# Attention and two MLPs on one core: unit 1's weight split taken out of the attention periods, first loads ahead of the branch

## The chip, the cores and the metric

One NeuronCore of a Trainium2 chip runs the whole program. The metric is the device time of one launch in microseconds (us). Engine names: PE is TensorE (PEld its weight loads), DVE is VectorE, ACT is ScalarE, POOL is GpSimd, SP is SyncE, which here only issues DMAs. A name with a q at its end (PEldq, SPq) is the engine's sequencer, or the DMA issues of its queue.

## The reference, cut to what matters

```python
# attention: batch 2, 12 heads, 448 tokens, head_dim 64, cap = 30
scores = (q @ k.T) / sqrt(64)
scores = cap * tanh(scores / cap)
attn = exp(scores - max(scores)); attn = attn / (sum(attn) + 1e-9)
x = attn @ v                                   # reshaped to 896 x 768
# first MLP, 768 -> 768 -> 768
x = max(x @ w1, x @ w2, x @ w3) @ moe_w_out
# second MLP, 768 -> 1536 -> 768
xn = x / sqrt(mean(x * x) + 1e-6) * rms_g
out = (silu(xn @ w_gate) * (xn @ w_val)) @ moe2_w_out
```

## The kernel before

The program reads the bits of `cap` into a register of every engine (line 630) and branches on them (line 631). With a cap of at most 40 the bounded variant runs, which needs no maximum of the scores; this is the variant in the trace.

**Attention** works on 12 pairs of heads (6 pairs in each of 2 batches), one after the other in `period(i)`, a software pipeline. In period i: SP loads pair i+2; DVE finishes the sum of pair i-1 (`sum_2`, L246), after `norm(i-2)` (the reciprocal, L270, and the product xs, L272), and then writes x of pair i-2 as a high and a low part (`split_x`, L280 and L281); PE computes the transposed scores of pair i (L220, L226), the products with V of pair i-1 (`values`, L260), and the row sums of pair i-1 by a product with ones (`sum_all`, L266); ACT takes tanh of the scores (L222, L229) and then their exponentials (`expo`, L233, two instructions). POOL begins the sum of exponentials (`sum_01`, L237, and `sum_3`, two instructions on L242) as soon as ACT has the exponentials; DVE does this for pairs 0 and 11. Each engine runs its instructions in the order in which the code wrote them. PE can begin the scores of pair i+1 only behind `sum_all(i-1)`, which waits for DVE's `sum_2(i-1)`, which waits for POOL's sums of pair i-1.

**The MLPs** are matmuls in float32r with each operand in two parts. Weights come as 60 units of 128 x 768. Each unit is loaded twice by SP (`raw`, and `mid`, the same bytes shifted by two), and DVE and ACT make a high and a low part of it in eight steps (`split_unit`, L109 to L117), after which the next unit's loads are issued. In attention only units 0 to 2 are split: unit 0 in period 0 in one piece, all on DVE; unit 1 by a list `steps`, of which periods 2 to 8 emit one step each, behind `split_x`, and period 9 the rest; unit 2 in `tail`. `tail` runs as a hook inside the first MLP group, after its 18 matmuls: it is period 12 (the last values and sums), the split of unit 2, and the norm and split of the last pair. Three groups on batch 0 (units 0, 1, 2) follow each other, then three on batch 1. From there on a table by group numbers says when each later unit is split.

**At the start**, behind the branch, ACT loads cap, SP loads K and Q of pair 0, DVE clears a tile, PE multiplies it with itself three times (L329, 448 columns each), and ACT runs one exponential, which loads the table.

Of the kernel before, what the change touches and what calls it, by code (L numbers as in the profile page):

```python
# [1 line left out]

# [16 lines left out]
B, H, S, D = 2, 12, 448, 64  # L19
NP = H // 2  # L20
P = 128
# [8 lines left out]
NT = B * S  # L30
NS = NT // P
U = 768
# [4 lines left out]
CAP_BITS = 0x42200000  # L37


@with_exitstack  # L40
def attn_moe_kernel(ctx, tc, bounded, qT, kT, v, cap, w123, wo, wgv, wo2, rms_g, out):
    nc = tc.nc
    pe, dve, act, pool, sp = nc.tensor, nc.vector, nc.scalar, nc.gpsimd, nc.sync

    const = ctx.enter_context(tc.tile_pool(name="const", bufs=1))
    gp = ctx.enter_context(tc.tile_pool(name="gp", bufs=1))
    wp = ctx.enter_context(tc.tile_pool(name="wp", bufs=1))
    tp = ctx.enter_context(tc.tile_pool(name="tp", bufs=1))
    pp = ctx.enter_context(tc.tile_pool(name="pp", bufs=1, space=PSUM))

    NG, NE, NT, NX = 28, 6, 6, 3

    BATCH, WIDE = (slice(0, S), slice(S, B * S)), (slice(0, 512), slice(512, B * S))
    AHEAD, SPACE, T_MIN = 3, 2, 2
# [2 lines left out]
        return gp.tile([P, 2, S], dt, tag="g", name=name, bufs=NG)  # L57

    def small(name, dt=F32):
        return tp.tile([P, 512], dt, tag="t", name=name, bufs=NT)  # L60

    def flat(name, in_quad=False):

# [11 lines left out]
    def bank():  # L75
        return pp.tile([P, 512], F32, tag="b", name="bank", bufs=5)
# [15 lines left out]

    def load_unit(src):
        raw = wp.tile([P, U, 2], U32, tag="raw", name="raw", bufs=2)
        mid = wp.tile([P, U, 2], U32, tag="mid", name="mid", bufs=2)
        sp.dma_start(out=raw.rearrange("p a b -> p (a b)"), in_=src.bitcast(U32))
        sp.dma_start(out=mid.rearrange("p a b -> p (a b)").bitcast(U16)[:, :4 * U - 2], in_=src.bitcast(U16)[:, 1:4 * U - 1])
        return raw[:, :, 1], mid[:, :, 0]  # L100

    def split_unit(words, on_dve, defer=None):
        hi, lo = (gp.tile([P, U], F32R, tag="g", name=name, bufs=NG) for name in ("whi", "wlo"))
        f = wp.tile([P, U], U32, tag="f", name="f", bufs=2)
        d = wp.tile([P, U], U32, tag="d", name="d", bufs=1)
        high, mid = words
        ff = f.bitcast(F32)
        steps = [
            (lambda: dve.tensor_scalar(f, high, 0x7FFFFFFF, None, op0=ALU.bitwise_and)) if on_dve else  # L109
            (lambda: act.activation(ff, high.bitcast(F32), AF.Abs)),  # L110
            lambda: dve.tensor_scalar(ff, ff, W_MIN, W_MAX, op0=ALU.max, op1=ALU.min),  # L111
            lambda: dve.tensor_scalar(f, f, 3, 0x3FFFF000, op0=ALU.logical_shift_left, op1=ALU.bitwise_and),  # L112
            lambda: dve.scalar_tensor_tensor(f, high, 0xC0000000, f, op0=ALU.bitwise_and, op1=ALU.bitwise_or),  # L113
            lambda: (dve.tensor_copy if on_dve else act.copy)(hi, ff),  # L114
            lambda: dve.tensor_scalar(d, f, 0xFF800000, None, op0=ALU.bitwise_and),
            lambda: dve.tensor_scalar(mid, mid, 0x01FFFFFF, None, op0=ALU.bitwise_and),
            lambda: dve.scalar_tensor_tensor(lo, mid, 2.0 ** -36, d.bitcast(F32), op0=ALU.mult, op1=ALU.mult),  # L117
            load_next,
        ]
        if defer is None:  # L120
            for step in steps:
                step()
        else:
            defer.extend(steps)
        return hi, lo

    unit_src = [w123[j, n] for j in range(KC) for n in range(3)]
# [1 line left out]
    unit_src += [wgv[f, n] for f in range(FC) for n in range(2)]  # L129
    unit_src += [wo2[half, k2] for half in range(2) for k2 in range(FC // 2)]  # L130
    U_WO, U_GV, U_O2 = 3 * KC, 4 * KC, 4 * KC + 2 * FC
    loaded, units = [], []

    def load_next():
        if len(loaded) < len(unit_src):
            loaded.append(load_unit(unit_src[len(loaded)]))

    def split_next(defer=None):
        i = len(units)
        units.append(split_unit(loaded[i], i < 2, defer))  # L140
        loaded[i] = None

    with tc.manual_schedule():

        pairs = [(b, hp) for b in range(B) for hp in range(NP)]
        n = len(pairs)
        kq, vt, E, EX, Ssum, SB, PO, XS, done = {}, {}, {}, {}, {}, {}, {}, {}, {}
# [8 lines left out]
        def load_pair(i):  # L156

            b, hp = pairs[i]
            k_, qv = tp.tile([P, S], F32, tag="k", name="k", bufs=3), big("qv")
            kq[i], vt[i] = (k_, qv[:, 0]), qv[:, 1]  # L160
            sp.dma_start(out=k_, in_=kT[b, hp])
            sp.dma_start(out=qv[:, 0], in_=qT[b, hp])
# [105 lines left out]
        def norm(i):  # L268
            r = small("r")[:, :S]
            dve.reciprocal(r, SB.pop(i)[:, :S])  # L270
            xs = XS[i] = spare()
            dve.tensor_mul(xs, PO.pop(i)[:, :S], r)  # L272

        def split_x(i):
            b, hp = pairs[i]
            if b == 0:
                X[hp] = flat("x")
            hi, lo = (t[:, BATCH[b]] for t in X[hp])
            xs = XS.pop(i)
            dve.tensor_copy(hi, xs)  # L280
            dve.tensor_sub(lo, xs, hi.bitcast(F32))  # L281
# [32 lines left out]
                two_parts(t, *(h[:, cols] for h in HT[j]))  # L314


        cap_sb = const.tile([P, 1], F32, name="cap_sb")
        g_sb = const.tile([P, KC], F32, name="g_sb")
        tsc = const.tile([P, 1], F32, name="tsc")
        act.dma_start(out=cap_sb, in_=cap.to_broadcast([P, 1]))  # L320
        load_pair(0)


        warm = small("warm")[:, :S]
        dve.memset(warm, 0.0)
        act.activation(tsc, warm[:, :1], AF.Exp)
        ps = bank()
        for _ in range(3):
            pe.matmul(ps[:, :S], warm[:, :P], warm, start=True, stop=True)  # L329
        load_next()  # L330
        load_pair(1)
        load_v(0)
# [11 lines left out]
        if bounded:  # L344

            guard = const.tile([P, 1], F32, name="guard")
            dve.tensor_scalar_mul(guard, cap_sb, -1.0)
            dve.tensor_tensor(guard, guard, cap_sb, op=ALU.min)
            act.activation(guard, guard, AF.Exp)
            dve.tensor_scalar_mul(guard, guard, 1e-9 / P)  # L350
            steps = []

            def period(i):

                if i + 2 < n:
                    load_pair(i + 2)
                    load_v(i + 2)
                if i >= 2:  # L360
                    norm(i - 2)
                if i == n:
                    sum_3(i - 1, dve)
                if i >= 1:
                    sum_2(i - 1)
                if i >= 2:
                    split_x(i - 2)

                    if i == 2:
                        split_next(steps)  # L370
                    for step in steps[:1 if i < 9 else None]:
                        step()
                    del steps[:1 if i < 9 else None]
                if i == 1:
                    scores(1, 0)
                    scores(1, 1)
                    values(0, 0, 1)
                    scores(1, 2)
                    scores(1, 3)
                    values(0, 2)  # L380
                    sum_all(0)
                else:
                    if i < n:
                        for c in range(NC):
                            scores(i, c)
                    if i >= 1:
                        values(i - 1, *(() if i < n else (3,)), 0, 1, 2)
                        sum_all(i - 1)
                if i < n:
                    expo(i)  # L390
                    if i == 0:

                        split_next()
                        sum_01(i, dve)
                        sum_3(i, dve)
                    else:
                        sum_01(i, dve if i == n - 1 else pool)
                        if i < n - 1:
                            sum_3(i, pool)

            def tail():
                period(n)
                split_next()
                norm(n - 1)
                split_x(n - 1)

            for i in range(n):
                period(i)
        else:
            for i in range(n):  # L410
                if i + 2 < n:
                    load_pair(i + 2)
                    load_v(i + 2)
                attend(i)
            for _ in range(3):
                split_next()
# [220 lines left out]
```

## Time and profile before

| | us |
|---|---|
| median of 3 runs | 552.27 (549.04 to 552.77) |
| profiled execution | 551.83 |
| its span in the trace | 550.0 |
| PE busy | 530.8 (97%) |
| DVE busy | 423.2 (77%) |
| ACT busy | 240.3 (44%) |
| POOL busy | 61.3 (11%) |

The span begins and ends inside the launch, 1.83 us shorter than it. Attention reaches from 0 to about 103 us, the MLPs from there to the end. Busy time counts an instruction from its begin to its end, its waiting for a port included. PE's busy time is that of overlapping instructions, so that a busy PE may still be slow.

### The profile page before, as it was taken

How to read it: one execution, taken by the hardware profiler on the slowest of the kernel's cores; microseconds unless marked ns; L12 is line 12 of the kernel's file. 1: busy time of each engine (PE TensorE's matmuls, PEld its weight loads, DVE VectorE, ACT ScalarE, POOL GpSimd, SP SyncE). 2: the span in 40 equal slices, each digit the busy share in tenths (PEclk: the TensorE clock that was granted, in tenths of full speed). 3: DMA queues.
4: the chain of work that ended last, by engine and by line, in shares of the span. 5: the costliest groups of instructions: out<-in, count | busy, mean ns of one | idle time of the engine just before them, and what ended most of it. 6: DMA issues, size and time to landing. Idle time of an engine off the chain costs nothing.

```text
span 550.0 us, 7028 instructions
## 1 busy us (share of the span) xinstructions
PE 530.8 (97%) x2684; PEld 436.0 (79%) x2684; DVE 423.2 (77%) x592; ACT 240.3 (44%) x347; POOL 61.3 (11%) x48
## 2 busy tenths in 40 slices
PE   7996996999999999999999999999999999999996
PEld 3332332489988889988998999998888899999996
DVE  4699999999898898776686888887877778836701
ACT  4996895523434333435454343333333333312301
POOL 0367367000000000003122000000000000000000
PEclk9999999999999999999999999999999999999999
DMA  7932231048897878676400587666666666974402
GB/s 251 371 104 71 86 122 59 0 121 282 297 333 286 283 241 280 234 258 229 141 0 1 174 260 238 221 212 213 208 207 222 227 222 209 327 275 168 162 1 106
DMA packets 24809, 105.89 MB, mean 193 GB/s; under 512 B 3008, under 2 KB 9408, under 8 KB 24768
## 3 DMA queue, kind: packets, MB, share of 16 engines
q1 hardware_dynamic: 23760, 104.19, 55.7%
q10 hardware_dynamic: 1008, 1.18, 0.6%
q8 instruction: 23, 0.38, 0.3%
q14 instruction: 18, 0.15, 0.1%
HBM read 102.60 MB, written 2.75 MB: 192 GB/s over the span
## 4 chain that ended last, share of the span: by engine, by line
PE 87%; DVE 6%; ACT 5%; POOL 1%; issue 1%; DVEq 0%; POOLq 0%
PE bank L290 40%; PE banko L290 16%; PE bank L558 10%; PE banks L290 7%; PE banko L558 3%; ACT e L222 3%; PE bank L220 2%; PE banks L558 2%; ACT e L233 2%; PE banko L260 2%; DVE sum L246 2%; DVE r L270 2%; PE banks L266 1%; PE bank L329 1%; DVE x L280 1%
## 5 line engine op out<-in xcount | busy, mean ns | idle before, releaser
L114 ACT CAST whi<-f 128x768 fp32r<-128x768 f32 x58 | 48.8, 841 | 148.4 <-DVE f L113 139.1
L290 PE MATMUL bank<-xn,whi 128*128 128x512 f32 (+1 forms) x360 | 102.9, 367 | 0.0
L290 PE MATMUL bank<-x,whi 128*128 128x512 f32 (+2 forms) x276 | 79.2, 368 | 0.0
L290 PEld LDWEIGHTS bank<-xn,whi 128*128 128x128 f32 x360 | 66.5, 188 | 8.2
L290 PE MATMUL bank<-xn,wlo 128*128 128x512 f32 (+1 forms) x180 | 66.2, 368 | 0.0
L117 DVE SCALAR_TENSOR_TENSOR wlo<-mid,d 128x768 fp32r<-128x768 uint32 x60 | 58.5, 974 | 3.1 <-PE bank L290 0.6
L113 DVE SCALAR_TENSOR_TENSOR f<-raw,f 128x768 uint32<-128x768 uint32 x60 | 57.5, 959 | 2.1
L290 PEld LDWEIGHTS bank<-x,whi 128*128 128x128 f32 x276 | 51.0, 188 | 7.4 <-ACT e L233 0.7
L110 ACT ACTIVATE f<-raw 128x768 f32<-128x768 f32 x58 | 52.5, 906 | 5.2 <-DMA raw<-in_wo 3.4
L558 PE MATMUL bank<-whi,a 128*128 128x384 f32 x216 | 54.8, 334 | 0.0
L111 DVE TENSOR_SCALAR f<-f 128x768 f32<-128x768 f32 x60 | 36.7, 612 | 19.1 <-ACT f L110 18.3
L290 PE MATMUL bank<-x,wlo 128*128 128x512 f32 (+2 forms) x138 | 50.8, 368 | 0.0
L222 ACT ACTIVATE e<-bank,tsc 128x448 f32<-128x448 f32 x72 | 39.2, 655 | 15.8 <-PE bank L220 15.5
L260 PE MATMUL banko<-e,qv 128*64 128x448 f32 (+1 forms) x192 | 40.7, 552 | 0.5 <-ACT e L233 0.5
L290 PE MATMUL banko<-xn,whi 128*128 128x512 f32 (+1 forms) x144 | 40.7, 364 | 0.0
L558 PEld LDWEIGHTS bank<-whi,a 128*128 128x128 f32 x216 | 39.0, 188 | 0.0
L233 ACT ACTIVATE e<-e,cap_sb 128x1792 f32<-128x1792 f32 (+1 forms) x24 | 37.7, 1652 | 0.0
L220 PE MATMUL bank<-qv,k 64*128 64x448 f32 x144 | 36.2, 587 | 1.2 <-DMA qv<-in_qT 0.6
L290 PEld LDWEIGHTS bank<-xn,wlo 128*128 128x128 f32 x180 | 33.8, 188 | 4.0
L270 DVE RECIPROCAL r<-banks 128x448 f32<-128x448 f32 x12 | 35.4, 2949 | 1.8 <-PE banks L266 1.8
L112 DVE TENSOR_SCALAR f<-f 128x768 uint32<-128x768 uint32 x60 | 34.6, 576 | 2.0
L558 PE MATMUL bank<-wlo,a 128*128 128x384 f32 x108 | 36.1, 334 | 0.0
(130 smaller groups left out, 891.1 us busy)
## 6 DMA issues: line engine op xcount, KB each, us to landing
raw<-in_wgv SPq DMA_DIRECT2D x24, 768.0 KB, 4.2
mid<-in_wgv SPq DMA_DIRECT2D x24, 767.5 KB, 5.3
raw<-in_w SPq DMA_DIRECT2D x18, 768.0 KB, 6.0
raw<-in_wo SPq DMA_DIRECT2D x18, 768.0 KB, 4.5
mid<-in_w SPq DMA_DIRECT2D x18, 767.5 KB, 5.9
mid<-in_wo SPq DMA_DIRECT2D x18, 767.5 KB, 5.6
k<-in_kT SPq DMA_DIRECT2D x12, 224.0 KB, 2.6
qv<-in_qT SPq DMA_DIRECT2D x12, 224.0 KB, 3.0
```

What stands on the lines that cost most here:

```text
L110: (lambda: act.activation(ff, high.bitcast(F32), AF.Abs)),
L111: lambda: dve.tensor_scalar(ff, ff, W_MIN, W_MAX, op0=ALU.max, op1=ALU.min),
L113: lambda: dve.scalar_tensor_tensor(f, high, 0xC0000000, f, op0=ALU.bitwise_and, op1=ALU.bitwise_or),
L114: lambda: (dve.tensor_copy if on_dve else act.copy)(hi, ff),
L117: lambda: dve.scalar_tensor_tensor(lo, mid, 2.0 ** -36, d.bitcast(F32), op0=ALU.mult, op1=ALU.mult),
L220: pe.matmul(ps[j][:, :S], k_[rows, c * P:(c + 1) * P], q_[rows], start=True, stop=True)
L222: act.activation(t[:, j, :], ps[j][:, :S], AF.Tanh, scale=tsc)
L233: act.activation(e, e, AF.Exp, scale=cap_sb)
L260: pe.matmul(PO[i][64 * j:64 * j + 64, :S], w, e, start=first, stop=(done[i] == NC))
L270: dve.reciprocal(r, SB.pop(i)[:, :S])
L290: pe.matmul(ps, a[:, k, :], x[k][h][:, cols], start=(k == 0 and n_ == 0), stop=(k == KC - 1 and n_ == 2))
L558: pe.matmul(acc_o[s][:, :HN], a[:, ts], w[:, sl], start=(k == 0 and n_ == 0), stop=(k == FC - 1 and n_ == 2))
```

## The change

There are two parts.

**The start.** Pools are made outside the kernel function, and a new function `begin` runs ahead of the read of `cap` and the branch. It holds the load of cap, K and Q of pair 0 (K now in two pieces: the first 128 columns, then, behind Q, the other 320), the clearing of the tile, the exponential that loads the table, and the warm-up matmuls, now of 448, 448 and 112 columns.

**The periods.** The list for unit 1 gives its first four steps to DVE in period 1, together with the load of the next `raw`, which is now issued right behind the last step that reads the old one; periods 2 to 11 have no step. The rest (the copy of the high part, now on ACT, and three steps on DVE) is written in period 12, ahead of `sum_2(11)`. POOL makes the first sums of pair 11 too. `split_x(10)` moves from period 12 to behind `norm(11)`.

```diff
+def begin(tc, pools, qT, kT, cap):
...
+    with tc.manual_schedule():
+        nc.scalar.dma_start(out=cap_sb, in_=cap.to_broadcast([P, 1]))
+        k_ = tp.tile([P, S], F32, tag="k", name="k", bufs=3)
+        qv = gp.tile([P, 2, S], F32, tag="g", name="qv", bufs=NG)
+        nc.sync.dma_start(out=k_[:, :P], in_=kT[0, 0][:, :P])
+        nc.sync.dma_start(out=qv[:, 0], in_=qT[0, 0])
+        nc.sync.dma_start(out=k_[:, P:], in_=kT[0, 0][:, P:])
...
+        for m in (S, S, S // 4):
+            nc.tensor.matmul(ps[:, :m], warm[:, :P], warm[:, :m], start=True, stop=True)
...
+        on_dve = first or defer is not None
...
-            lambda: (dve.tensor_copy if on_dve else act.copy)(hi, ff),
+            lambda: (dve.tensor_copy if first else act.copy)(hi, ff),
...
-            load_next,
+            load_mid,
         ]
+        steps.insert(4, load_raw)
...
                 if i == n:
-                    sum_3(i - 1, dve)
+                    for step in steps:
+                        step()
                 if i >= 1:
                     sum_2(i - 1)
-                if i >= 2:
+                if i == 1:
+                    split_next(steps)
+                    for step in steps[:5]:
+                        step()
+                    del steps[:5]
+                if 2 <= i < n:
                     split_x(i - 2)
-                    if i == 2:
-                        split_next(steps)
-                    for step in steps[:1 if i < 9 else None]:
-                        step()
-                    del steps[:1 if i < 9 else None]
...
-                        sum_01(i, dve if i == n - 1 else pool)
-                        if i < n - 1:
-                            sum_3(i, pool)
+                        sum_01(i, pool)
+                        sum_3(i, pool)
             def tail():
                 period(n)
                 split_next()
                 norm(n - 1)
+                split_x(n - 2)
                 split_x(n - 1)
...
+        begun = begin(tc, pools, named["qT"], named["kT"], named["cap"])
         cap_bits = nc.values_load(args[list(arrays).index("cap")].bitcast(I32))
         with tc.If((cap_bits & 0x7FFFFFFF) <= CAP_BITS) as small_cap:
```

**Where instructions move.** PE at the start of the program, before and then in the change (`in_cap` is the read of cap into a register, `warm` the cleared tile):

```order
L630 TENSOR_LOAD in_cap_ptr
L630 TENSOR_LOAD in_cap
L631 REGISTER_ALU
L631 COMPARE_AND_BRANCH
L329 MATMUL bank<-warm 128x448 x3
L220 MATMUL bank<-qv,k 128x448 x6
```

```order
L73 MATMUL bank<-warm 128x448 x2
L73 MATMUL bank<-warm 128x112
L662 TENSOR_LOAD in_cap_ptr
L662 TENSOR_LOAD in_cap
L663 REGISTER_ALU
L663 COMPARE_AND_BRANCH
L258 MATMUL bank<-qv,k 128x448 x6
```

The warm-up stands ahead of the two register loads and the branch, which now lie between it and the first scores.

DVE from `sum_2(0)` to the second split of x, before (rows with L109 and L111 are steps of unit 1; in each of the next periods one more stands behind L281) and then in the change (L284 is `sum_2`, L308 the reciprocal, L318 and L319 the split of x):

```order
L246 SCALAR_TENSOR_TENSOR sum<-e_141,guard,sum 128x896
L270 RECIPROCAL r<-banks 128x448
L272 TENSOR_TENSOR xs<-banko,r 128x448
L246 SCALAR_TENSOR_TENSOR sum<-e_193,guard,sum 128x896
L280 CAST x<-xs 128x448
L281 TENSOR_TENSOR x<-xs,x 128x448
L109 TENSOR_SCALAR f<-raw 128x768
L270 RECIPROCAL r<-banks 128x448
L272 TENSOR_TENSOR xs<-banko,r 128x448
L246 SCALAR_TENSOR_TENSOR sum<-e_254,guard,sum 128x896
L280 CAST x<-xs 128x448
L281 TENSOR_TENSOR x<-xs,x 128x448
```

```order
L284 SCALAR_TENSOR_TENSOR sum<-e_145,guard,sum 128x896
L146 TENSOR_SCALAR f<-raw 128x768
L148 TENSOR_SCALAR f<-f 128x768
L149 TENSOR_SCALAR f<-f 128x768
L150 SCALAR_TENSOR_TENSOR f<-raw,f 128x768
L308 RECIPROCAL r<-banks 128x448
L310 TENSOR_TENSOR xs<-banko,r 128x448
L284 SCALAR_TENSOR_TENSOR sum<-e_207,guard,sum 128x896
L318 CAST x<-xs 128x448
L319 TENSOR_TENSOR x<-xs,x 128x448
L308 RECIPROCAL r<-banks 128x448
L310 TENSOR_TENSOR xs<-banko,r 128x448
```

Four steps now stand together between `sum_2(0)` and the first reciprocal, and the reciprocal of each later period follows the split of x directly.

DVE at the end of attention, from the norm of pair 10 on, before and then in the change (L237 and L242 are the first sums of pair 11; L115 to L117, in the change L152 to L154, are the last steps of a unit):

```order
L237 TENSOR_TENSOR sum<-e_750 128x896
L270 RECIPROCAL r<-banks 128x448
L272 TENSOR_TENSOR xs<-banko,r 128x448
L242 TENSOR_TENSOR sum<-sum,e_751 64x448 x2
L246 SCALAR_TENSOR_TENSOR sum<-e_751,guard,sum 128x896
L280 CAST x<-xs 128x448
L281 TENSOR_TENSOR x<-xs,x 128x448
L111 TENSOR_SCALAR f<-f 128x768
```

```order
L308 RECIPROCAL r<-banks 128x448
L310 TENSOR_TENSOR xs<-banko,r 128x448
L152 TENSOR_SCALAR d<-f 128x768
L153 TENSOR_SCALAR mid<-mid 128x768
L154 SCALAR_TENSOR_TENSOR wlo<-mid,d 128x768
L284 SCALAR_TENSOR_TENSOR sum<-e_749,guard,sum 128x896
L148 TENSOR_SCALAR f<-f 128x768
```

The two kinds of first sums are gone from DVE (POOL has them), three steps of unit 1 stand ahead of `sum_2(11)`, and the split of x of pair 10 has left its place behind it.

## Rows read from the trace of the kernel before

**Rows 1.** The page's chain that ended last: share of the span by engine.

```profile
PE 87%; DVE 6%; ACT 5%; POOL 1%; issue 1%; DVEq 0%; POOLq 0%
```

**Rows 2.** That chain in order of time: start, length (us), engine, tile, line.

```profile
50.45 2.28 DVE sum L246
52.87 1.76 PE banks L266 x4
54.63 3.53 PE bank L220 x12
...
103.30 3.84 PE bank L290 x18
```

**Rows 3.** Timeline, ACT's exponentials of pairs 2 to 7 and 11: start, length.

```profile
26.00 3.23 ACT L233 ACTIVATE e<-e,cap_sb 128x1792 f32<-128x1792 f32 x2
...
32.87 3.13 ACT L233 ACTIVATE e<-e,cap_sb 128x1792 f32<-128x1792 f32 x2
...
39.80 3.13 ACT L233 ACTIVATE e<-e,cap_sb 128x1792 f32<-128x1792 f32 x2
...
47.72 3.13 ACT L233 ACTIVATE e<-e,cap_sb 128x1792 f32<-128x1792 f32 x2
...
60.09 3.13 ACT L233 ACTIVATE e<-e,cap_sb 128x1792 f32<-128x1792 f32 x2
...
66.90 3.13 ACT L233 ACTIVATE e<-e,cap_sb 128x1792 f32<-128x1792 f32 x2
...
101.16 3.13 ACT L233 ACTIVATE e<-e,cap_sb 128x1792 f32<-128x1792 f32 x2
```

**Rows 4.** Timeline, DVE beside POOL, and a step at the end of attention.

```profile
34.84 2.09 POOL L237 TENSOR_TENSOR sum<-e 128x896 f32<-128x896 f32 x1 [2.02 <-ACT e L233]
34.89 2.45 DVE L111 TENSOR_SCALAR f<-f 128x768 f32<-128x768 f32 x1
...
41.84 2.28 DVE L280 CAST x<-xs 128x448 fp32r<-128x448 f32 x1
...
111.00 0.56 DVE L111 TENSOR_SCALAR f<-f 128x768 f32<-128x768 f32 x1
```

**Rows 5.** Groups by line: count, busy us, mean ns, idle before.

```profile
L117 DVE SCALAR_TENSOR_TENSOR wlo<-mid,d 128x768 fp32r<-128x768 uint32 x60 | 58.5, 974 | 3.1 <-PE bank L290 0.6
L270 DVE RECIPROCAL r<-banks 128x448 f32<-128x448 f32 x12 | 35.4, 2949 | 1.8 <-PE banks L266 1.8
...
L242 POOL TENSOR_TENSOR sum<-sum,e 64x448 f32<-64x448 f32 x20 | 25.2, 1258 | 1.5
```

**Rows 6.** The start: sequencer records (ns, first and last start), timeline, landing of Q.

```profile
L630 PEldq TENSOR_LOAD <-in_cap_ptr x1: 911/911/911, 0.8 to 0.8; - x1
L631 PEldq COMPARE_BRANCH  x2: 95/1922/3749, 2.5 to 542.1; - x2
2.56 0.43 DVE L325 MEMSET warm<- 128x448 f32 x1 [2.56 <-issue]
3.14 4.82 PE L329 MATMUL bank<-warm 128*128 128x448 f32 x6 [3.14 <-DVE warm L325]
7.89 2.98 PE L220 MATMUL bank<-qv,k 64*128 64x448 f32 x12
9.16 3.26 ACT L222 ACTIVATE e<-bank,tsc 128x448 f32<-128x448 f32 x6 [1.59 <-PE bank L220]
9.29 0.56 DVE L109 TENSOR_SCALAR f<-raw 128x768 uint32<-128x768 uint32 x1 [1.53 <-DMA raw<-in_w]
qv<-in_qT SPq DMA_DIRECT2D x1, 224.0 KB, 4.3
```

**Rows 7.** Timeline: DVE's `sum_2(0)`, POOL's first sum, PE's last `sum_all`.

```profile
17.25 1.15 DVE L246 SCALAR_TENSOR_TENSOR sum<-e,guard,sum 128x896 f32<-128x896 f32 x1
...
21.37 2.08 POOL L237 TENSOR_TENSOR sum<-e 128x896 f32<-128x896 f32 x1 [18.38 <-ACT e L233]
...
110.27 0.97 PE L266 MATMUL banks<-sum,ones 128*64 128x448 f32 x4
```

More of the change, by code (lines that the diff above doesn't have):

```diff
@@ L1 @@
 import struct
+from contextlib import ExitStack
 import concourse.bass as bass
@@ L5 @@
 from concourse import mybir
-from concourse._compat import with_exitstack
 from concourse.masks import make_identity
@@ L37, with make_pools @@
 CAP_BITS = 0x42200000
[L40 to L43, printed above, removed]
+NG, NE, NTMP, NX = 28, 6, 6, 3
+def make_pools(ctx, tc):
     const = ctx.enter_context(tc.tile_pool(name="const", bufs=1))
@@ L49, in attn_moe_kernel @@
     pp = ctx.enter_context(tc.tile_pool(name="pp", bufs=1, space=PSUM))
-    NG, NE, NT, NX = 28, 6, 6, 3
+    return const, gp, wp, tp, pp
+def begin(tc, pools, qT, kT, cap):
+    nc = tc.nc
+    const, gp, wp, tp, pp = pools
+    cap_sb = const.tile([P, 1], F32, name="cap_sb")
+    tsc = const.tile([P, 1], F32, name="tsc")
+    with tc.manual_schedule():
[5 more added lines that the diff above has]
+        nc.sync.dma_start(out=k_[:, P:], in_=kT[0, 0][:, P:])
+        warm = tp.tile([P, 512], F32, tag="t", name="warm", bufs=NTMP)[:, :S]
+        nc.vector.memset(warm, 0.0)
+        nc.scalar.activation(tsc, warm[:, :1], AF.Exp)
+        ps = pp.tile([P, 512], F32, tag="b", name="bank", bufs=5)
+        for m in (S, S, S // 4):
+            nc.tensor.matmul(ps[:, :m], warm[:, :P], warm[:, :m], start=True, stop=True)
+    return cap_sb, tsc, k_, qv
+def attn_moe_kernel(tc, pools, begun, bounded, qT, kT, v, cap, w123, wo, wgv, wo2, rms_g, out):
+    nc = tc.nc
+    pe, dve, act, pool, sp = nc.tensor, nc.vector, nc.scalar, nc.gpsimd, nc.sync
+    const, gp, wp, tp, pp = pools
+    cap_sb, tsc, k_0, qv_0 = begun
     BATCH, WIDE = (slice(0, S), slice(S, B * S)), (slice(0, 512), slice(512, B * S))
@@ L59, in small @@
     def small(name, dt=F32):
-        return tp.tile([P, 512], dt, tag="t", name=name, bufs=NT)
+        return tp.tile([P, 512], dt, tag="t", name=name, bufs=NTMP)
     def flat(name, in_quad=False):
@@ L89, in any_bank, with load_raw, load_mid, split_unit @@
         return (bank_s if turn[0] == 0 else bank_o if turn[0] in (3, 6) else bank)()
[L95 to L102, printed above, removed]
+    def load_raw():
+        if len(raws) < len(unit_src):
+            raw = wp.tile([P, U, 2], U32, tag="raw", name="raw", bufs=2)
+            sp.dma_start(out=raw.rearrange("p a b -> p (a b)"), in_=unit_src[len(raws)].bitcast(U32))
+            raws.append(raw[:, :, 1])
+    def load_mid():
+        if len(mids) < len(unit_src):
+            mid = wp.tile([P, U, 2], U32, tag="mid", name="mid", bufs=2)
+            sp.dma_start(out=mid.rearrange("p a b -> p (a b)").bitcast(U16)[:, :4 * U - 2], in_=unit_src[len(mids)].bitcast(U16)[:, 1:4 * U - 1])
+            mids.append(mid[:, :, 0])
+    def split_unit(high, mid, first, defer=None):
         hi, lo = (gp.tile([P, U], F32R, tag="g", name=name, bufs=NG) for name in ("whi", "wlo"))
@@ L105, in split_unit @@
         d = wp.tile([P, U], U32, tag="d", name="d", bufs=1)
-        high, mid = words
         ff = f.bitcast(F32)
+        on_dve = first or defer is not None
         steps = [
@@ L131, in attn_moe_kernel @@
     U_WO, U_GV, U_O2 = 3 * KC, 4 * KC, 4 * KC + 2 * FC
-    loaded, units = [], []
+    raws, mids, units = [], [], []
     def load_next():
-        if len(loaded) < len(unit_src):
-            loaded.append(load_unit(unit_src[len(loaded)]))
+        load_raw()
+        load_mid()
     def split_next(defer=None):
         i = len(units)
-        units.append(split_unit(loaded[i], i < 2, defer))
-        loaded[i] = None
+        units.append(split_unit(raws[i], mids[i], i < 1, defer))
     with tc.manual_schedule():
@@ L314, in w123_gemm @@
                 two_parts(t, *(h[:, cols] for h in HT[j]))
-        cap_sb = const.tile([P, 1], F32, name="cap_sb")
         g_sb = const.tile([P, KC], F32, name="g_sb")
[L319 to L329, printed above, removed]
+        kq[0], vt[0] = (k_0, qv_0[:, 0]), qv_0[:, 1]
         load_next()
@@ L628 @@
     o = nc.dram_tensor("out", (NT, DM), F32, kind="ExternalOutput").ap()
-    with tile.TileContext(nc) as tc:
+    with tile.TileContext(nc) as tc, ExitStack() as ctx:
+        pools = make_pools(ctx, tc)
+        named = dict(zip(arrays, args))
+        begun = begin(tc, pools, named["qT"], named["kT"], named["cap"])
         cap_bits = nc.values_load(args[list(arrays).index("cap")].bitcast(I32))
         with tc.If((cap_bits & 0x7FFFFFFF) <= CAP_BITS) as small_cap:
-            attn_moe_kernel(tc, True, *args, o)
+            attn_moe_kernel(tc, pools, begun, True, *args, o)
         with small_cap.Else():
-            attn_moe_kernel(tc, False, *args, o)
+            attn_moe_kernel(tc, pools, begun, False, *args, o)
     r = run_bass_kernel_spmd(nc, [{f"in_{n}": a for n, a in arrays.items()}], core_ids=[0])
```

## The prediction

> **What bounds the kernel now.** I read the page's chain first. PE carries 87% of it, DVE and ACT 11% [rows 1]; so the question is where the chain leaves PE. In order of time it does so before 103.30 us only; from there PE's matmuls follow each other nearly to the end [rows 2], and nothing that the change does after attention can shorten them. What can be won lies in the first 103 us.
>
> There I read ACT's exponentials, since each period has exactly one pair of them. From 60.09 to 66.90 a period takes 6.81 us. From 39.80 to 47.72 it takes 7.92 and from 47.72 to 60.09 it takes 12.37; the four periods from 66.90 to 101.16 take 34.26, 7.0 more than four of 6.81 [rows 3]. So two stalls of 6.7 and 7.0 us stand among nine periods. The chain says how one arises: `sum_2` ends at 52.73, PE's `sum_all` can only then begin, it and the next scores run slowly after PE's idle time (1.76 and 3.53 us), and ACT waits for those scores [rows 2].
>
> Why `sum_2` is late is read from DVE beside POOL. At 34.84 POOL begins a sum of 2.09 us. At 34.89 DVE begins a step of the weight split that takes 2.45 us, where the same step takes 0.56 us at 111.00, with POOL idle [rows 4]. It ends 0.4 us after POOL's sum: DVE waited for it. The lost 1.9 us put the next `split_x` behind POOL's next start (its cast takes 2.28 us at 41.84), and then `sum_2` itself (2.28 us at 50.45, where it is 1.15 us alone) [rows 2, 4, 7]. One step that meets POOL thus costs a stall two periods later.
>
> **The change: no steps in periods 2 to 11.** DVE's work of a period is then the reciprocal of 2.95 us [rows 5], the product, `sum_2` (1.15, [rows 7]) and the split of x, under 6 us of 6.81, and of it only `sum_2` and the split of x meet POOL. POOL's three instructions last 2.08 + 2 x 1.26 = 4.6 us at the most [rows 5, 7], so they leave 2.2 us of a period, in which `sum_2` and the split fit. I take all nine periods from pair 2 to pair 11 at 6.81: 61.3 us where 75.16 stand now [rows 3]. Gain **13.9**. Its upper bound is about that, since ACT is busy through such a period; its lower bound is in the rivals.
>
> **Four steps in period 1.** `sum_2(0)` ends at 18.40 and POOL's first sum begins at 21.37 [rows 7], a hole of 2.97 us. The steps take 3 x 0.56 and one like L117's kind, 0.97 at the most [rows 4, 5]: 2.7 us with their gaps, done at about 21.15. The reciprocal behind them moves a microsecond later, but the `sum_2(1)` that follows it waits for POOL until 25.9 in any case. Cost 0, as long as ACT and DVE move by nearly the same amount at the start: POOL begins when ACT is done, and the steps when DVE is. The last step starts 1.2 us before POOL does; that is the margin. The `raw` load that SP issues behind these steps holds up the loads of pair 4 by 3 us, and those are used more than ten microseconds later. Cost 0.
>
> **The tail.** Count from T, the start of the last exponentials (101.16 now). POOL begins pair 11's sums at T + 1.95, as it does at 34.84 after exponentials that start at 32.87 [rows 3, 4], and ends at T + 6.5. DVE comes out of the norm of pair 10 before that, waits for POOL until T + 6.5, makes three steps (0.56 + 0.56 + 0.97, [rows 4, 5]) and `sum_2(11)` (1.15): done at T + 9.75. `sum_all(11)` begins at T + 9.1 now (110.27, [rows 7]). Cost **0.6**. Bounds: 0, if a step gets in between two of POOL's instructions, and 2, if POOL is held up for the length of the steps. Unit 2's split then starts later by the same 0.6, less the 1.0 us of `split_x(10)` that has left its way; x of pair 10 and 11 are wanted five and six k-steps into the fourth group, more than 1 us after they are done. Cost 0.
>
> **The start.** Now the read of cap begins at 0.8 and DVE's first instruction stands at 2.56: 1.8 us for the branch. The warm-up runs from 3.14 to 7.9, the first scores start at 7.89 and the first tanh at 9.16 [rows 6]. In the change DVE clears the tile at about 1.0, PE's warm-up starts at 1.6 and needs 4 passes of 0.8 us and two short ones: it ends at 5.3. Q, issued at 1.2 and 4.3 us on its way [rows 6], lands at 5.5. What remains open is the branch on PE. If PE reads cap while the matmuls run, only the branch is left: the one at the program's end takes 3.75 us on PE, from 542.1 until the last matmul is out [rows 6], so it waits for PE to be empty, and the scores start at 5.9. If the reads wait as well, 1.8 us more: 7.1. Against 7.89 that is a gain of 2.0 or 0.8. I take **1.6**, nearer to the first, because the record at 542.1 shows PE's sequencer 3 us ahead of its matmuls. ACT's table and cap are there before the first tanh in both cases.
>
> **A rule against the shorter warm-up.** The row shows a warm-up of 4.82 us and scores that run at full speed soon after it (12 passes in 2.98 us, against 3.53 after the stall at 52.87) [rows 2, 6]. The Trainium skill, "TensorE: Matmul & The Clock Gate", "Part 1: The HAM clock gate", says that an idle TensorE is held at the lower of its two clocks until it has been kept busy for a while. By that rule, with a warm-up about a quarter shorter and a gap behind it, the first scores would run at 1.2 GHz. By the rows that costs between 0.55 us (3.53 less 2.98) and 0.8 (1.76 less 0.97 for one `sum_all`, [rows 2, 7]); it is a rival below.
>
> **The sum.** 551.83 - 13.9 + 0.6 - 1.6 = 536.9 for the profiled execution; the median of the runs is 0.44 above that execution, so 537.3.
>
> **Rivals.**
>
> 1. *Period 1 meets POOL.* If ACT gains 1.6 at the start but DVE less than 0.5, POOL's first sum begins before the last of the four steps, and DVE falls behind by a step as at 34.89. For it: unit 0's split starts when its `raw` lands, 9.29 [rows 6], and that load is now issued behind three other issues and the branch, so it may come no earlier. Against: the loads ahead of it start 1.5 us earlier and free the queues. The price is one stall as above, 7.92 + 12.37 - 2 x 6.81 = 6.7 us: **544.0**. Chance 0.16. The Trainium skill, "SBUF — State Buffer", "Who interferes with whom", states that whichever of the two engines starts first keeps the shared port for its whole instruction; the 2.45 us at 34.89 agree with it.
> 2. *Lower clock in the first scores*, 0.8 us: **538.1**. Chance 0.12.
> 3. *The change doesn't do what it says.* The stalls belong to the rhythm of POOL and DVE, not to the steps. For it: the second stall ends in a period that had no step left. Against: the delay that leads to each begins at a step. Both would stay: 551.8 + 0.6 - 1.6 + 0.4 = **551.2**. Chance 0.05.
> 4. *Slower.* DVE falls behind in period 1 and does not recover: in every period the split of x, written behind `sum_2`, meets POOL. It decides once `sum_2` starts more than 0.9 us later than now, since the split then begins after POOL. The periods would alternate between 7.92 and 12.37, nine of them 91.3 us in place of 75.16: 552.3 + 16.1 + 0.6 - 1.6 = **567**. Against it: after 60.09 the next period is clean at once, because the stall of ACT delays POOL too. Chance 0.03.
>
> The forecast itself has 0.62; the remaining 0.02 is for what I don't see.
>
> **How the numbers follow.** The predicted time is 537.3. Its own range is 533.5 to 540: down by the upper bounds of start and tail (0.4 and 0.6) and the spread of the runs (the lowest of before is 3.2 below the median), up by the lower bound of the start (0.8), the upper one of the tail (1.4) and a little of the spread. The range given reaches to 545, to hold the first rival. One per cent, 5.5 us, is about what a measurement of this kernel tells from no change. Forecast, rivals 1 and 2 lie beyond it: faster 0.92. Rival 3 is within: 0.05. Slower 0.03.
>
> **What would show it.** Exponentials of pairs 2 to 11 about 6.8 us apart, all of them; no cast or `sum_2` on DVE over 2 us between 25 and 90; the last exponentials starting near 85.7 instead of 101.16. The first scores near 6 us, the first tanh near 7.5. The last `sum_all` 9.7 us after the last exponentials. The MLPs as long as before. A period over 8 us between pair 2 and pair 6 would show rival 1; first scores at 7 or later would show that PE reads cap behind its matmuls; an MLP stage longer by a microsecond or more would mean that something here costs later, and the sum would lack a term.

## The result, and the profile after

The change takes 544.37 us in the median (12 runs, 542.73 to 545.53). The kernel before, run beside it, takes 548.76 (12 runs, 546.35 to 553.46). The ratio is 0.990, with a 95% interval of 0.9865 to 0.9935: about one per cent faster. The prediction was 537.3, in a range of 533.5 to 545.0. The profiled execution of the change takes 544.5 us, its span 542.7; that of before had 551.83 and 550.0. So the span is 7.3 us shorter, where the prediction's terms make 14.9.

The median lies inside the range only because the range was stretched to 545 for the first rival, whose price gave 544.0. That the two times are close is luck: the stall of that rival did not happen, as the next rows show.

Attention first. The exponentials of ACT after the change (start, length), of pairs 0 to 3 and of pair 11:

```profile
9.85 3.13 ACT L271 ACTIVATE e<-e,cap_sb 128x1792 f32<-128x1792 f32 x2
19.14 3.10 ACT L271 ACTIVATE e<-e,cap_sb 128x1792 f32<-128x1792 f32 x2
25.76 3.15 ACT L271 ACTIVATE e<-e,cap_sb 128x1792 f32<-128x1792 f32 x2
32.53 3.13 ACT L271 ACTIVATE e<-e,cap_sb 128x1792 f32<-128x1792 f32 x2
...
87.07 3.13 ACT L271 ACTIVATE e<-e,cap_sb 128x1792 f32<-128x1792 f32 x2
```

From pair 2 to pair 11 they take 61.31 us, where [rows 3] have 75.16: 13.85 gained, and every period is 6.7 to 6.8 us. But pair 2 starts at 25.76 where it started at 26.00, only 0.24 earlier, although pair 0 starts 2.95 us earlier (9.85, then 12.80).

The start, PE's rows of the timeline and ACT's first tanh:

```profile
1.39 3.76 PE L73 MATMUL bank<-warm 128*128 128x448 f32 x6 [1.39 <-DVE warm L69]
...
5.08 2.83 PE L258 MATMUL bank<-qv,k 64*128 64x448 f32 x12
...
6.21 3.26 ACT L260 ACTIVATE e<-bank,tsc 128x448 f32<-128x448 f32 x6 [1.02 <-PE bank L258]
...
7.84 0.97 PE L264 MATMUL bank<-qv,k 64*64 64x448 f32 x4
...
11.52 2.84 PE L258 MATMUL bank<-qv,k 64*128 64x448 f32 x8 [2.71 <-DMA qv<-in_qT]
...
14.29 2.30 PE L298 MATMUL banko<-e,qv 128*64 128x448 f32 x8
```

The first scores come at 5.08 and take 2.83 us, no longer than before the change [rows 6]. Then PE waits 2.71 us for Q of pair 1. Behind that wait 8 score passes take 2.84 us; 12 had taken 2.83 before it. In the kernel before, the same 8 passes took 1.77 us, behind a shorter wait for the same load:

```profile
12.40 1.77 PE L220 MATMUL bank<-qv,k 64*128 64x448 f32 x8 [0.63 <-DMA qv<-in_qT]
```

The granted clock of these stretches (stretch, length, then busy time and count of PE, PEld, DVE, ACT, POOL, then PEclk, DMA share, GB/s):

```profile
8.80:11.50 2.70, 0.01 (x2) 0.01 (x1) 2.56 (x5) 2.70 (x4) 0.00 (x0) 1.00 1.02 394
11.50:13.40 1.90, 1.88 (x7) 1.01 (x8) 1.87 (x4) 1.90 (x4) 0.00 (x0) 0.66 1.04 433
13.40:15.00 1.60, 1.60 (x6) 0.29 (x4) 1.50 (x3) 1.30 (x4) 0.00 (x0) 0.50 0.98 407
15.00:16.50 1.50, 1.50 (x8) 0.38 (x4) 1.45 (x3) 0.49 (x1) 0.00 (x0) 0.83 1.02 373
```

The clock falls to 0.50, which is 1.2 of 2.4 GHz, behind the wait. (It reads 1.00 during the wait, when PE does nothing.)

The steps in period 1, and the tail (timeline of DVE, POOL, PE):

```profile
18.90 0.96 DVE L150 SCALAR_TENSOR_TENSOR f<-raw,f 128x768 uint32<-128x768 uint32 x1
...
21.03 2.09 POOL L275 TENSOR_TENSOR sum<-e 128x896 f32<-128x896 f32 x1 [16.77 <-ACT e L271]
...
96.67 0.97 PE L304 MATMUL banks<-sum,ones 128*64 128x448 f32 x4 [0.32 <-DVE sum L284]
```

The fourth step ends at 19.86, 1.2 us ahead of POOL. The last row sums begin at 96.67, 9.60 us after the last exponentials, where [rows 3, 7] have 9.11. Both as predicted.

Then the MLPs. I count them from the group of 18 matmuls after the tail, which begins at 111.24 before and at 97.65 now. Before they take 550.0 - 111.24 = 438.8 us, now 542.7 - 97.65 = 445.05: **6.3 us longer**, where the prediction had "as long as before". In this stage the chain of waits after the change, in order of time, leaves PE at one place (start, length, engine, tile, line):

```profile
210.91 7.11 PE bank L328 x35
218.04 0.96 DVE wlo L154
219.92 0.58 ACT m L345
...
232.20 0.70 DVE h L335
232.95 0.73 PE bank L328 x2
233.68 5.72 PE banko L328 x18
239.40 4.09 PE bank L328 x18
```

From 210.91 to 239.40 are 28.49 us. The same 108 matmuls of the kernel before follow each other, from 224.16 to 246.90, 22.74 us:

```profile
224.16 7.27 PE bank L290 x36
231.43 4.12 PE banko L290 x18
235.55 7.27 PE bank L290 x36
242.82 4.08 PE banko L290 x18
246.90 4.08 PE bank L290 x18
```

So 5.75 of the 6.3 us lie here. The timeline of DVE and PE in this place, after the change:

```profile
218.04 0.96 DVE L154 SCALAR_TENSOR_TENSOR wlo<-mid,d 128x768 fp32r<-128x768 uint32 x1 [3.38 <-PE bank L328]
...
232.22 0.50 PE L328 MATMUL bank<-h,whi 128*128 128x512 f32 x1 [3.34 <-ACT h L334]
...
232.95 0.50 PE L328 MATMUL bank<-h,whi 128*128 128x512 f32 x1 [0.23 <-DVE h L335]
```

DVE waits 3.38 us for PE before it can write the low part of a weight unit. From there it works nearly without a gap and is still late at 230.78, when it takes the maximum that becomes h; PE waits 3.34 us for h. Then the clock falls a second time, and the next 18 matmuls take 5.72 us where 4.08 is usual:

```profile
228.00:232.00 4.00, 0.88 (x4) 0.38 (x3) 3.32 (x6) 1.29 (x2) 0.00 (x0) 1.00 0.86 281
232.00:235.00 3.00, 2.56 (x8) 1.87 (x9) 2.62 (x4) 0.98 (x2) 0.00 (x0) 0.83 0.82 306
235.00:238.00 3.00, 3.00 (x10) 2.34 (x9) 2.62 (x5) 1.05 (x2) 0.00 (x0) 0.61 0.55 184
```

Over the whole span the page's chain is PE to 92%, where [rows 1] have 87%.

### The profile page after: what moved, and what is told of

It is laid out like the page before. It is cut to its first block, busy times and chain, and to the rows that moved or that the text cites. A ratio compares the mean times of both kernels' runs of the same rounds, so it can differ in the third digit from the quotient of the medians.

```text
span 542.7 us, 7046 instructions
## 1 busy us (share of the span) xinstructions
PE 529.6 (98%) x2684; PEld 436.9 (81%) x2684; DVE 405.4 (75%) x588; ACT 241.6 (45%) x348; POOL 62.5 (12%) x51
## 4 chain that ended last, share of the span: by engine, by line
PE 92%; DVE 3%; ACT 1%; DMA 1%; SPq 1%; issue 1%; DVEq 0%; ACTq 0%
PE bank L328 39%; PE banko L328 16%; PE bank L587 10%; PE banks L328 7%; PE bank L258 5%; PE banko L298 5%; PE banko L587 3%; PE banks L587 2%; PE bank L264 2%; PE banks L304 2%; DMA qv<-in_qT 1%; ACT e L271 1%; DVE r L308 1%; DVE d L152 0%; DVE m L347 0%
## 5 line engine op out<-in xcount | busy, mean ns | idle before, releaser
L154 DVE SCALAR_TENSOR_TENSOR wlo<-mid,d 128x768 fp32r<-128x768 uint32 x60 | 57.5, 959 | 7.9 <-PE bank L328 4.8
L148 DVE TENSOR_SCALAR f<-f 128x768 f32<-128x768 f32 x60 | 34.9, 581 | 17.3 <-ACT f L147 16.5
L308 DVE RECIPROCAL r<-banks 128x448 f32<-128x448 f32 x12 | 35.5, 2957 | 4.3 <-PE banks L304 4.3
L152 DVE TENSOR_SCALAR d<-f 128x768 uint32<-128x768 uint32 x60 | 34.3, 571 | 2.0
```

## The theory, and its rival

Which buffer a tile gets is read from the built program. A tag names a set of equal buffers that tiles take in turn; a buffer is free again when the last user of its tile is done. The tag `g` has 28 buffers. `qv` (Q and V of a pair), the sums of exponentials, the parts of x and h, and the high and low parts of weight units all take the next one that is free. In the change `qv` of pair 0 is made in `begin`, ahead of the branch, and **used in both branches**. It is never given back: its buffer holds nothing else to the program's end, where in the kernel before six further tiles use it in turn. (K of pair 0, one of three buffers, has the same fate.) With one buffer less the weight units slip against the buffers. Unit 21 (counted from 0) is the one that waits at 218.04. In the kernel before, its two parts take the buffers of the two parts of unit 15, which the 32nd group of the MLPs is the last to read. In the change the low part takes the buffer of the high part of unit 16, which the 34th group still reads, two groups later.

**Theory 1**: this one pinned buffer makes the MLP 6.3 us longer. **Rival 1**: something else in the order (unit 1's and unit 2's splits, `split_x(10)`, the loads' phase). **Theory 2**, on the start: the clock that falls behind the wait for Q of pair 1 takes the gain. **Rival 2**: the landing of Q alone decides.

## Experiments

**Own tiles.** The change, with the two tiles out of the rotations:

```diff
-        k_ = tp.tile([P, S], F32, tag="k", name="k", bufs=3)
-        qv = gp.tile([P, 2, S], F32, tag="g", name="qv", bufs=NG)
+        k_ = const.tile([P, S], F32, name="k")
+        qv = const.tile([P, 2, S], F32, name="qv")
```

> The change, with K and Q of pair 0 in two tiles of their own instead of one buffer each out of the rotations. Theory 1 (a pinned buffer): in the change Q of pair 0 keeps one of the 28 buffers of tag g for the whole program, because both branches use it, so the low part of a weight unit must wait for matmuls two groups later; with the tile outside the rotation the first MLP runs as before, from the second group's start to the end of the span about 438.8 us in place of 445.1, and the time is 538 to 539.5. The wait of 3.4 us for PE that the low part has at 218 us is gone, and the stretch of 3.3 us idle PE near 229 us with it. Rival 1 (the MLP is longer because the work around unit 1 and unit 2 is written in another order, or because the loads have another phase): nothing of that changes here, the MLP keeps its 445, the time is 544 to 545.

Measured: 538.35 us (6 runs), ratio to before 0.982 (0.976 to 0.987). The MLP takes 536.5 - 97.61 = 438.9. In the built program the low part of unit 21 follows unit 15 and the 32nd group again. DVE's longest wait before a low part, and PE's groups in the chain, now without a gap:

```profile
217.81 0.96 DVE L154 SCALAR_TENSOR_TENSOR wlo<-mid,d 128x768 fp32r<-128x768 uint32 x1 [0.77 <-PE bank L328]
```

```profile
210.50 7.27 PE bank L328 x36
217.77 4.12 PE banko L328 x18
221.89 7.27 PE bank L328 x36
229.16 4.08 PE banko L328 x18
233.24 4.08 PE bank L328 x18
```

The two tiles in the rotation cost the whole 6 us; every instruction is written in the same order as in the change.

**The periods alone.** `begin` is called inside the kernel function, per branch, so nothing is shared:

```diff
-        nc.sync.dma_start(out=k_[:, :P], in_=kT[0, 0][:, :P])
+        nc.sync.dma_start(out=k_, in_=kT[0, 0])
...
-        nc.sync.dma_start(out=k_[:, P:], in_=kT[0, 0][:, P:])
...
-        for m in (S, S, S // 4):
+        for m in (S, S, S):
...
-    cap_sb, tsc, k_0, qv_0 = begun
+    cap_sb, tsc, k_0, qv_0 = begin(tc, pools, qT, kT, cap)
...
-        begun = begin(tc, pools, named["qT"], named["kT"], named["cap"])
+        begun = None
```

> The change's periods and tail alone: the start stands behind the branch as in the kernel before, K in one load, three warm-up matmuls of 448 columns, so that no tile is shared by both branches. Theory 1: the MLP takes 438.8 us; the attention takes what it takes in the change plus 0.2 us, since the earlier start gave only that: 538 to 540. Rival 1: the written order of the MLP is that of the change, so the stall of about 6 us stays: 544 to 545.5.

Measured: 538.73 us (538.54 to 539.06), ratio 0.983 (0.977 to 0.989). The MLP takes 536.8 - 97.70 = 439.1. All exponentials from pair 1 to pair 11 are 6.6 to 6.9 apart. Without any of the early start the median is that of the version with own tiles (0.4 us apart, within the spread), so in most runs of that version the early start brought nothing. In the profiled executions pair 2 starts at 25.71 without it and at 25.72 with it.

**The start alone**, on the kernel before's periods and tail (the change with these put back; the cut shows the steps):

```diff
-                if i == 1:
-                    split_next(steps)
-                    for step in steps[:5]:
-                        step()
-                    del steps[:5]
-                if 2 <= i < n:
+                if i >= 2:
                     split_x(i - 2)
+                    if i == 2:
+                        split_next(steps)
+                    for step in steps[:1 if i < 9 else None]:
+                        step()
+                    del steps[:1 if i < 9 else None]
...
```

> The change's start alone, with the kernel before's periods and tail. Theory 1: the stalls of attention stay as in the kernel before (last exponentials near 100 us, give or take one stall of 6.7), and the MLP is about 6 us longer, since Q of pair 0 keeps its buffer: slower than the kernel before by 3 to 7 us, 552 to 556. Rival 1: the MLP's written order is that of the kernel before, so it takes 438.8: as fast as the kernel before or 0.2 us faster, 548 to 549.

Measured: 558.19 us (554.89 to 559.57), ratio 1.017 (1.011 to 1.023): more than expected. The MLP takes 556.7 - 111.83 = 444.9, with the same 3.38 us before the same low part:

```profile
231.87 0.96 DVE L148 SCALAR_TENSOR_TENSOR wlo<-mid,d 128x768 fp32r<-128x768 uint32 x1 [3.38 <-PE bank L321]
```

The written order of this MLP is that of the kernel before, so rival 1 falls here too. What I had missed: exponentials of pair 2 start at 24.14, 1.9 us earlier than before, yet the last ones at 101.74. With steps in the periods the head start is lost in more stalls. And what bears on theory 2: the start is that of the change, Q of pair 1 lands at the same time, and here the start does bring its 1.9 us to pair 2. The first scores take longer (3.70 us), the wait for Q is therefore shorter (1.87), and the granted clock is 1.00 in every stretch to 25 us:

```profile
5.08 3.70 PE L251 MATMUL bank<-qv,k 64*128 64x448 f32 x12
...
11.55 1.77 PE L251 MATMUL bank<-qv,k 64*128 64x448 f32 x8 [1.87 <-DMA qv<-in_qT]
```

**One buffer less**, on the version with the periods alone:

```diff
-NG, NE, NTMP, NX = 28, 6, 6, 3
+NG, NE, NTMP, NX = 27, 6, 6, 3
```

> As the run with the periods and tail alone (start behind the branch), but the tag g has 27 buffers instead of 28; no tile is shared by the branches. Theory 1: one buffer less in the rotation is what the pinned tile does, so the first MLP gets stalls where the low part of a unit waits for PE: 543 to 546, 4 to 7 us over the run with 28. Rival 1: the number of buffers does not decide, the time is that of the run with 28 within 1 us.

Measured: 544.72 us (12 runs, 544.08 to 545.47), 6.0 over the run with 28; MLP 542.3 - 97.54 = 444.8. The low part of unit 21 again follows unit 16 and the 34th group, and the row is that of the change:

```profile
217.56 0.96 DVE L152 SCALAR_TENSOR_TENSOR wlo<-mid,d 128x768 fp32r<-128x768 uint32 x1 [3.38 <-PE bank L326]
```

So one buffer less does it without a pinned tile, and giving it back undoes it. Theory 1 stands from both sides. The buffer of K plays no part that shows: here all three of that tag are in turn.

**A full warm-up**, on own tiles, to shorten PE's wait for Q of pair 1:

```diff
-        for m in (S, S, S // 4):
+        for m in (S, S, S):
```

> The version with K and Q of pair 0 in tiles of their own, with three warm-up matmuls of 448 columns instead of 448, 448 and 112. There PE now waits 2.28 us for Q of pair 1 before the second scores, and the granted clock is 0.87, 0.50 and 0.56 from 11.5 to 16.5 us; the second exponentials start 8.87 us after the first. Theory 2 (the start's gain is lost to the clock that falls behind that wait, not to the wait itself): the longer warm-up ends near 6.1 and the first scores end a microsecond later, so PE waits 1.4 to 1.9 us only, the granted clock stays 1.00, the second exponentials start at 17.3 to 17.8 instead of 19.11, and a longer warm-up makes the kernel faster: 536.5 to 537.3 where the version with own tiles has 538.35. Rival 2 (the landing of Q of pair 1 alone decides): the second exponentials stay at 19.1, 538.2 to 538.6. Rival 3 (with ACT earlier POOL meets the four steps in period 1): a period over 8 us between pairs 2 and 6, 540 to 545.

Measured: 537.23 us (536.86 to 538.55), ratio 0.977 (0.971 to 0.983). In the profiled execution (538.23) the warm-up ended at 5.53 only, PE waited 2.39 us, and the clock fell as before (0.51 from 11.5 to 13.4); the second exponentials started at 19.12. So its trace does not decide. The runs say more, by the mean granted clock of each. Here two of six have 0.994 or 0.995 and take 538.23 and 538.55; the other four have 0.998 to 1.000 and take 536.86 to 537.38, close to what theory 2 forecast. With own tiles and the short warm-up, five of six have 0.994 to 0.997 and take 538.09 to 538.73; the one at 1.000 takes 536.94. Where in a run the clock fell is known of the profiled ones only.

**A longer warm-up**, of four:

```diff
-        for m in (S, S, S // 4):
+        for m in (S, S, S, S):
```

> The version with K and Q of pair 0 in tiles of their own and four warm-up matmuls of 448 columns. With three, the warm-up ended at 5.5 and not at 6.1, PE still waited 2.39 us for Q of pair 1, and the clock of 11.5 to 15.0 was 0.51 in the profiled execution, so that the question of the wait was not put. With four the warm-up should end near 6.3, the first scores near 9.9, and the wait be 1.5 to 1.9 us, between the 0.91 and 1.87 us after which the clock stayed at 1.00 and the 2.28 us after which it fell. Theory 2 (the clock takes the start's gain): granted clock 1.00 from 11.5 to 16.5, second exponentials at 17.4 to 17.8, third near 24.2. The time is then 536.6 to 537.2 if DVE's split of x stays ahead of POOL, or 537.5 to 540 with two or three periods of 7.4 us as in the version with Q of pair 1 early, where it came 0.1 us after POOL. Rival 2 (the landing of Q alone): second exponentials at 19.1, 538.2 to 538.6.

Measured: 537.63 us (537.26 to 538.73), ratio 0.978 (0.973 to 0.984); the profiled execution has 537.26. PE's wait for Q is 1.16 us, and the clock stays:

```profile
11.52 1.77 PE L258 MATMUL bank<-qv,k 64*128 64x448 f32 x8 [1.16 <-DMA qv<-in_qT]
```

```profile
11.50:13.40 1.90, 1.88 (x10) 0.89 (x12) 1.86 (x4) 1.90 (x3) 0.00 (x0) 1.00 1.02 425
13.40:15.00 1.60, 1.60 (x9) 0.43 (x9) 1.50 (x3) 1.60 (x3) 0.00 (x0) 1.00 1.00 413
```

Q lands at the same 11.52, yet the second exponentials start at 18.01 (I expected 17.4 to 17.8) and the third at 24.62, 1.1 us earlier than with own tiles and the short warm-up (19.11 and 25.72). The profiled span is 1.0 shorter (535.5). So rival 2 falls in the traces: with Q at the same time, it is the clock. In the medians the difference (0.7) is within the spread of the runs: with a clock of 0.999 or 1.000 in all six, they still reach from 537.26 to 538.73, and that part is not explained.

**Q of pair 1 early**, on own tiles with the short warm-up:

```diff
-        load_next()
+        load_raw()
         load_pair(1)
+        load_mid()
         load_v(0)
```

> The version with K and Q of pair 0 in tiles of their own, with the loads of K and Q of pair 1 issued ahead of unit 0's second load (mid), the short warm-up kept. Q of pair 1 should land near 9.8 instead of 11.4, so PE waits 1 to 1.5 us before the second scores and the clock stays at 1.00. If nothing else is in the way, the second exponentials start near 16.6 instead of 19.11 and the time is 535.8 to 536.3. Rival: POOL's first sum then begins near 18.5, when one or two of the four steps in period 1 have not begun (they run from 17.1 to 19.9); such a step waits for POOL, takes over 2 us, and DVE falls behind: a period of about 8 us and one of 12 between pairs 2 and 6, 540 to 545. The prediction's first rival had this mechanism at 544.0.

Measured: 539.52 us (536.85 to 544.17), ratio 0.983 (0.976 to 0.990), between the two times expected; the two runs near 544 have no trace. PE waits 0.91 us for Q, the clock stays at 1.00, and exponentials of pair 2 start at 24.14, 1.6 us earlier. Then the periods take 7.4 to 7.5 us three times:

```profile
24.14 3.15 ACT L271 ACTIVATE e<-e,cap_sb 128x1792 f32<-128x1792 f32 x2
31.60 3.13 ACT L271 ACTIVATE e<-e,cap_sb 128x1792 f32<-128x1792 f32 x2
39.08 3.13 ACT L271 ACTIVATE e<-e,cap_sb 128x1792 f32<-128x1792 f32 x2
```

DVE and POOL show why:

```profile
19.35 0.96 DVE L150 SCALAR_TENSOR_TENSOR f<-raw,f 128x768 uint32<-128x768 uint32 x1
19.42 2.83 POOL L275 TENSOR_TENSOR sum<-e 128x896 f32<-128x896 f32 x1 [15.19 <-ACT e L271]
...
26.13 2.09 POOL L275 TENSOR_TENSOR sum<-e 128x896 f32<-128x896 f32 x1 [1.46 <-ACT e L271]
26.20 2.50 DVE L319 TENSOR_TENSOR x<-xs,x 128x448 fp32r<-128x448 f32 x1
```

The fourth step starts at 19.35, 0.07 us ahead of POOL, which then needs 2.83 us instead of 2.08; one period later the split of x comes 0.07 us after POOL and takes 2.50 instead of 0.62. This is close to the prediction's first rival, in the place where the start does gain, but with the roles exchanged: the last step comes just ahead of POOL and holds POOL up, and the price is 0.6 to 0.7 us in each of three periods, not one stall of 6.7. The Trainium skill, "SBUF — State Buffer", "Who interferes with whom", says that a DVE instruction with two inputs in SBUF contends with a POOL instruction that reads there; this difference of two tiles, 2.50 us beside POOL, agrees.

**The kernel before, four more executions**, unchanged, because its runs lie in clusters:

> The kernel before, unchanged, to see whether the stalls of its attention vary from run to run: its runs lie in two clusters, near 546 and near 552.5. If the stalls are what varies, a run near 546 has its last exponentials near 95 (one stall of 6.7 us less than the 101.16 of the profile shown), a run near 552 has them near 101, and the MLP takes 438.8 in either. If the attention is the same in all runs, the last exponentials start at 101.2 and the MLP differs.

> The same as the other run of the unchanged kernel before: a second look, last exponentials near 95 with a time near 546, or near 101 with a time near 552, and an MLP of 438.8 us in both cases; or the same attention in both, if the stalls do not vary.

> The kernel before, a third look for an execution near 546 us: with one stall of 6.7 us less in attention (last exponentials near 95) and an MLP of 438.8 to 439.4 us if the stalls vary from run to run; near 552 with the last exponentials at 101 to 102 if this is the slower kind again, as the first three profiled executions were.

> The same as the third look at the kernel before: last exponentials near 95 with a time near 546, or near 101 with a time near 552, and the MLP at 438.8 to 439.4 us in either.

Measured: 552.62, 553.17, 548.69 and 546.54 us, with the last exponentials at 101.19, 101.93, 95.89 and 95.09, and MLPs of 439.4, 439.0, 439.4 and 439.6. The last of them:

```profile
60.17 3.10 ACT L233 ACTIVATE e<-e,cap_sb 128x1792 f32<-128x1792 f32 x2
...
95.09 3.14 ACT L233 ACTIVATE e<-e,cap_sb 128x1792 f32<-128x1792 f32 x2
```

The first stall is in all four (12.3 to 13.0 us to the exponentials at 59.8 to 60.2); the second, of 7 us, is whole in two, 1.5 us in one (95.89) and gone in one; by the times (551.6 us and more), 21 of the 51 runs of this kernel that stand beside the change and the experiments have it. The execution that the prediction was made from has both.

## Why the prediction was wrong

- **The periods, 13.9: right**, 13.85. The version with the periods alone shows that no stall stays without steps, against the prediction's third rival. A part of its size belongs to the execution: a run near 546 has only about 7 us of stalls to lose. So the gain over the median of before was bound to be smaller than forecast: before was put at 552.27 and was 548.76 in the comparison, 3.5 us less. The predicted time does not suffer from it, since without stalls both kinds of execution end alike.
- **The tail, 0.6: right**, 0.5 (10.58 us from the last exponentials to the next group, 97.65 - 87.07, before 111.24 - 101.16 = 10.08).
- **Four steps in period 1, 0: right**, but with little room. With 1.6 us gained at the start the collision is there.
- **The start, 1.6: wrong**, 0.24. Each step up to the first tanh was right or better: PE reads `cap` while its matmuls run (its branch stands at 4.0, the warm-up ends at 5.15), and the first tanh came at 6.21, not 7.5. What failed is the step from there to the end: I took ACT's shift at pair 0 as a shift of everything, and never asked when Q of pair 1 lands. Its row of before was there to be read, the wait of PE for that DMA at 12.40. The load lands at 11.52 now, 0.9 earlier, and PE is 3 us earlier. The wait is 2.71, and the clock behind it takes more than another microsecond. It is the clock that takes the gain and not the wait alone: with Q at 11.55 and the clock at 1.00, the start alone had its 1.9 us at pair 2. The prediction's second rival, a lower clock, had the right mechanism; in the change it struck in another place, at the second scores. The prediction's rule against the shorter warm-up is about the first scores, and there the change alone says little: they took 2.83 us, against 2.76 with three or four full matmuls, but with the same start 3.24 (own tiles), 3.64 (Q early) and 3.70 (the start alone). In the last of these their weight loads stand 0.75 us apart at first, as in the warm-up, where the change has 0.38; the granted clock of the profile reads 1.00 in all of them, so that the rows do not name the cause.
- **"The MLPs as long as before": wrong**, 6.3 us longer. From "nothing that the change does after attention can shorten them" I went on as if they could not get longer either: I asked what the change could give there, and not what it could take. The prediction named the sign of this, an MLP stage longer by a microsecond or more, and it came. The term that the sum lacked is no instruction at all: a tile allocated earlier, and used in both branches, keeps a buffer. Own tiles bring the stage back to 438.9 us, and one buffer less alone makes it 444.8. (In the unchanged kernel's five traces it takes 438.8 to 439.6, so that 5.5 to 6.3 us is what the traces bear.) Of the 6.3, PE's waits are 3.57 and the slow 18 matmuls behind them 1.6; 0.3 lie in matmuls that ran 2% slower between 97 and 117 us. One execution of the unchanged kernel (548.69) has these too, so they are not the change's; their cause is open, and the rest I did not place.

The terms as they came: -13.85 + 0.5 - 0.24 + 6.3 = -7.3, which is 550.0 to 542.7. The failure is in the last two, +6.3 and +1.4, together 7.7, against 544.5 - 536.9 = 7.6 of the profiled executions.

The version with own tiles and three or four full warm-up matmuls beats both kernels: 537.2 to 537.6 us, ratio 0.978 (0.973 to 0.984 for four). It is what the prediction expected of the change, about 537; with four, pair 2 starts 1.4 us earlier than before, and the nine periods behind it take 61.4 us. The periods alone, with nothing of the start, have 538.73.

## What to carry to other kernels

Of a tile that a change moves to an earlier place, ask not only when it is filled but when its buffer comes back: a value shared by both sides of a branch holds its buffer to the end, and the price can be due 200 us later, in a stage that the diff does not touch. When an operation comes earlier, follow the next one on that engine to what it waits for: here 2.95 us at the first tanh became 0.24 two pairs later. And look at several executions before you take a stall for the kernel's own; here one of two was in fewer than half of the runs.

## What the runs showed of the hardware

A wait of PE of 2.28, 2.39 or 2.71 us at the start, and of 3.34 at 228.9, was followed by stretches at a granted clock of 0.50 to 0.87; waits of 0.52 to 1.87 us in the same place, in nine other traces, were not (1.00 in all stretches to 16.5). Whether it is the length of the wait alone that decides, these traces do not separate. The Trainium skill, "TensorE: Matmul & The Clock Gate", "HAM oscillation — how this bites in real kernels", says that waits for DMA between short blocks of matmuls send TensorE back to its lower clock; the traces agree: behind the wait of 2.28 us the granted clock was 0.87, 0.50 and 0.56 in three stretches. A longer warm-up, which delays the first scores by 1.6 us, made the third exponentials 1.1 us earlier in the profiled execution: the wait was 1.16 us and the clock stayed at 1.00.

POOL and DVE fill a period almost completely: in the change's steady periods the split of x ends some 0.1 us before POOL's next sum starts (34.36 and 34.47 in the version with a full warm-up). That is why, with Q of pair 1 early, the 0.75 us by which one sum of POOL was longer (2.83 in place of 2.08) was enough for three long periods.
